# Clustered attention and a gated FFN on one core: Strassen's scheme for four more token tiles, the last product in parts, and 44 casts moved to GpSimd

## The chip, the cores and the metric

One core of a Trainium2 chip. The time is that of one execution on the device, in microseconds (us); a lower number is better. The core has five engines with an instruction queue each: TensorE (PE in the profile; its weight loads are shown apart as PEld), VectorE (DVE), ScalarE (ACT), GpSimd (POOL) and SyncE (SP), which in this kernel starts most DMAs. PE writes to PSUM, eight banks per partition; the other tiles lie in SBUF.

## The reference

The inputs are q, k and v of shape (4 batches, 8 heads, 768 tokens, 64), centroids of shape (8, 16, 64) and the three weight matrices of the FFN. All are float32, and so is the output of 3072 x 512.

```python
q_assign = argmax(q_n @ c_n.T, axis=-1)           # nearest of 16 centroids, by cosine
k_assign = argmax(k_n @ c_n.T, axis=-1)
mask     = q_assign[..., :, None] == k_assign[..., None, :]
scores   = where(mask, scale * q @ k.T, -1e9)
attn     = softmax(scores)                        # over the keys
x        = (attn @ v), heads side by side         # (3072, 512)
out      = (sigmoid(x @ w_gate) * (x @ w_val)) @ w_out   # 512 -> 1536 -> 512
```

So each batch has an attention part and an FFN part, and the last matrix product is (3072 x 1536) by (1536 x 512).

## The kernel before

**Attention.** For each pair of heads, k and q are split in two float16 parts: `hi` is the value cast to float16, and `lo` what the cast left out. The two lie side by side in a tile `hl`, which is turned (transposed) into `T`. In batch 0 and the first pair of batch 1 most of this is placed by hand and turned on PE. For the other eleven pairs (three of batch 1, four of batches 2 and 3 each) `pair_prep` does it: `sp(e, side)` makes `hl` of one head and side, with the cast on DVE (line 1353) and the subtraction on POOL (line 1354); `tn` turns `hl` by a DMA transpose on SP (line 410); `lg` multiplies `T` by the centroids on PE (line 434), `pk` picks the nearest on DVE (lines 449 to 469), and `ot` and `hp` bring the result back under `T` as 16 more rows, by DMAs on SP. Then one matmul of `T` against itself (`sc`, line 788, 384 queries wide) gives masked scores. ACT takes the exponential (`es`, line 793), and three matmuls multiply it by v (`av`, line 811). Such a group of one `sc` and three `av` is a step; there are 384 steps, 96 in each batch. At the end of a head DVE adds a correction and inverts the sum (`t`, `rec`, lines 370 and 372), POOL scales (`xp`, line 375), and a DMA transpose on SP writes `xTb` (line 842), the input of the FFN.

**FFN.** It runs in blocks of 384 tokens, two to a batch. For each of the 12 groups of 128 hidden units, a gate (`g`, line 529, four matmuls) and a value (`v`, line 545, four matmuls) are made; ACT takes tanh, and DVE joins both into `hT` (line 550). The output product has two forms. `plain_out` multiplies one tile of 128 tokens by the whole of w_out: 12 matmuls 512 wide (line 583), then one copy out of PSUM, on ACT or DVE, and one store. `product_out` takes two tiles (`t1`, `t2`) by Strassen's scheme in Winograd's form: instead of eight products of quarter matrices it makes seven, each of six matmuls 256 wide (line 716). It needs sums of the quarters of `hT` (`Sums.make`, lines 626 to 632, DVE, four for a pair) and differences of the quarters of w_out (`mix_wo`, line 276, DVE, eight operations in all). The differences overwrite the tiles `kheld`, `qheld` and `vheld`, which held batch 0's last pair of heads, and a quarter of w_out itself. Its results are added up from two PSUM banks `x` and `y`, which are filled in turn (`end1` to `end7`, line 658 on DVE, one on ACT at line 662). In batch 0 all six tiles go through `plain_out`; in batches 1 to 3 tiles (0, 1) are one pair, and tiles (3, 2) and (4, 5) are two pairs that go through one call.

**Order.** The order of all instructions is fixed when the program is built. `at` and `plan` put a piece of work at a step number plus an offset from the table `SCHED`. FFN matmuls are a queue of small pieces (atoms), each with a cost in ns; at each step `ffn_run(ns)` adds the step's allowance (`ns00` to `ns33`, batch and quarter of the batch) and issues atoms until it is used up. Each engine then runs its own list in order, and waits on semaphores where a tile is not ready or a buffer not free. `sc`, `g`, `v` and most logits share a ring of four PSUM banks; `x` and `y` are the two banks of the pool `op`. After the last step the rest of the queue runs without attention work beside it: the last block's gates and values, and then the product of tiles (3, 2) and (4, 5) of batch 3, with `final` set. In that last call the seven products run back to back, and the stores are made in two column halves, each over both pairs.

Of the kernel before, what the change touches and what calls it, by code (L numbers as in the profile page):

```python
# [98 lines left out]
def kernel(  # L99
# [415 lines left out]
    def ffn_atoms(xT, t0, n, b, final=False):  # L515
        blk = t0 // 384
        gv = []
        cost = NDC * max(n, 80) / 2.4 + 3
        pairs = [] if b < PB else [(0, 1)] if blk == 0 else [(3, 2), (4, 5)]
        sm = {x: Sums(b, *x) for x in pairs}  # L520

        def gate(fc, st):
            def f():
                need(("w", fc // WQ, 0), *(("x", b, p, t0 // 128 + c) for p in range(NP) for c in range(n // 128)))
                if fc == 0:
                    HB[b, blk] = htp.tile([128, NFC, 384], HP, name="hT")
                g = bank(512, name="g")
                for dc in range(NDC):
                    PE.matmul(  # L529
                        out=g[:, 0:n], lhsT=wg[fc // WQ][:, dc, fc % WQ, :],  # L530
                        rhs=xT[:, dc, t0 : t0 + n],
                        start=(dc == 0), stop=(dc == NDC - 1),
                    )
                th = thp.tile([128, 384], FP, name="th")
                ACT.activation(th[:, 0:n], g[:, 0:n], AF.Tanh)  # L535
                st.append(th)

            return f

        def val(fc, st):  # L540
            def f():
                need(("w", fc // WQ, 1))
                w = bank(512, name="v")
                for dc in range(NDC):
                    PE.matmul(  # L545
                        out=w[:, 0:n], lhsT=wv[fc // WQ][:, dc, fc % WQ, :],
                        rhs=xT[:, dc, t0 : t0 + n],
                        start=(dc == 0), stop=(dc == NDC - 1),
                    )
                DVE.scalar_tensor_tensor(  # L550
                    HB[b, blk][:, fc, 0:n], st[0][:, 0:n], 1.0, w[:, 0:n], ALU.add, ALU.mult
                )
                for k, x in SUMS_AT[b >= PB, blk].get(fc, []):
                    sm[x].make(k)
                if fc == NFC - 1 and pairs and blk == 0:
                    aside.extend(product_out(b, [sm[(0, 1)]], False))

            return f

        for fc in range(NFC):  # L560
            st = []
            gv.append((cost, gate(fc, st)))
            gv.append((cost, val(fc, st)))
        outs = []
        if b < PB:
            for t in range(n // 128):
                outs += plain_out(b, blk, t)
        elif blk == 1:
            outs = product_out(b, [sm[x] for x in pairs], final)
        return gv + outs  # L570

    def plain_out(b, blk, t):
# [3 lines left out]
        def outp(part):  # L576
# [22 lines left out]

    PB = 1  # L600
    SUMS_AT = {
        (False, 0): {}, (False, 1): {},
        (True, 0): {5: [(3, (0, 1))], 11: [(1, (0, 1)), (2, (0, 1))]},
        (True, 1): {
            1: [(1, (3, 2))], 5: [(2, (3, 2)), (3, (3, 2))], 6: [(3, (4, 5))],
            11: [(1, (4, 5)), (2, (4, 5))],
        },
# [26 lines left out]
    def product_out(b, sums, final):  # L634


        P_ = len(sums)
        st = {}

        def begin():  # L640
            need(*(("wo", i) for i in range(WOP)), *(("wt", i, c) for i in range(4) for c in range(2)))
            slot = taken["op"] % 2
            u = [out_bank() for _ in range(2)]
            x = 0 if slot != taken["last"] else 1
            taken["last"] = (slot + x) % 2
            taken["pair"] = True
            for z, t in (("x", u[x]), ("y", u[1 - x])):
                st[z] = t[:, 0 : P_ * HD].rearrange("p (e m) -> p e m", m=HD)
            if P_ == 1:
                ob = osp.tile([128, 2, DM], FP, name="ob")  # L650
                st["o1"], st["o2"] = ob[:, 0:1], ob[:, 1:2]
            else:
                st["o1"] = osp.tile([128, 2, DM], FP, name="ob")
                st["o2"] = osp.tile([128, 2, DM], FP, name="ob")
            for o in ("o1", "o2"):
                st[o, 0], st[o, 1] = st[o][:, :, 0:HD], st[o][:, :, HD:DM]

        plus = lambda dst, a, z: DVE.tensor_tensor(dst, a, z, ALU.add)  # L658
        C11, C12, C21, C22 = ("o1", 0), ("o1", 1), ("o2", 0), ("o2", 1)

        def end1():
            ACT.activation(st[C11], st["x"], AF.Copy)

        def end4():
            plus(st[C21], st["y"], st[C11])

        def end6():
            plus(st[C12], st["x"], st[C11])

        def end5():  # L670
            plus(st[C22], st["y"], st[C11])
            for m in sums:
                m.make(4)

        def end7():
            plus(st[C21], st["x"], st[C21])
            plus(st[C22], st["x"], st[C22])
            for i, m in enumerate(sums):
                store(st["o2"][:, i], b, m.t2, 1)

        def end3():
            plus(st[C12], st["y"], st[C12])
            if final:
                store(st[C12], b, sums[0].t1, P_, slice(HD, DM))

        def end2():
            plus(st[C11], st["x"], st[C11])
            taken["pair"] = False
            if final:
                store(st[C11], b, sums[0].t1, P_, slice(0, HD))  # L690
            else:
                store(st["o1"], b, sums[0].t1, P_)

        steps = [
            ("x", lambda m: tok(b, m.t1, 0), B11, True, end1),
            ("y", lambda m: tok(b, m.t2, 1), T4, True, end4),
            ("x", lambda m: m.of[2], T2, True, end6),
            ("y", lambda m: m.of[1], T1, True, end5),
            ("x", lambda m: m.of[3], T3, False, end7),
            ("y", lambda m: m.of[4], B22, False, end3),  # L700
            ("x", lambda m: tok(b, m.t1, 1), B21, True, end2),
        ]
        atoms = []
        G = SCHED.get("og", 3)

        def atom(k, e, g):
            z, lhs, rhs, start, end = steps[k]

            def f():
                if k + e + g == 0:  # L710
                    while aside and P_ > 1:
                        aside.pop(0)[1]()
                    begin()
                a = lhs(sums[e])
                for c in range(g, g + G):
                    PE.matmul(  # L716
                        out=st[z][:, e], lhsT=a[:, c, :], rhs=rhs[:, c, :],
                        start=start and c + e == 0, stop=c == HF - 1, skip_group_check=True,
                    )
                if g + G == HF and e == P_ - 1:  # L720
                    end()

            return f

        for k in range(7):
            for e in range(P_):
                for g in range(0, HF, G):
                    atoms.append((G * (HD / 2.4 + 2.5), atom(k, e, g)))
        return atoms

    queue = []
# [118 lines left out]
    def plan(name, step, f):  # L850
        at(SCHED.get(name, step), f)
# [489 lines left out]
        plan(f"wo{i}", 44 + 6 * i, lambda i=i: load_wo(i))  # L1341
    for i in range(4):
        for c in range(2):
            plan(f"wt{i}{c}", (150 + 8 * i if i < 3 else 200) + 4 * c, lambda i=i, c=c: mix_wo(i, c))

    def pair_prep(b, p, use):
        st = {}

        def sp(e, side):
            if side == 0:  # L1350
                st["hl", e] = hlp.tile([128, 12, 128], HP, tag="hl", name="hl")
            hl, r = st["hl", e][:, 6 * side : 6 * side + 6], RAW["kq"[side], b, p][:, e]
            DVE.tensor_copy(hl[:, :, 0:64], r)  # L1353
            POOL.tensor_tensor(hl[:, :, 64:128], r, hl[:, :, 0:64], ALU.subtract)  # L1354

        def lgt(e):
# [129 lines left out]
```

## Time and profile before

| | |
|---|---|
| median of 3 runs | 324.65 us (324.54 to 325.34) |
| the profiled execution | 324.9 us, of which 323.1 us are its span, from the first to the last instruction |
| PE busy | 314.7 us, 97% of the span |
| DVE busy | 226.7 us, 70% |
| ACT busy | 231.1 us, 72% |
| POOL busy | 108.6 us, 34% |
| TensorE clock granted | full speed in every slice |

A matmul's duration in the profile includes the time that it takes to run out of the array, so two matmuls overlap in the list: what one costs PE is the distance from its start to the start of the next. A bracket behind a row of a timeline says how long the engine was idle before it, and what released it. "x4" behind a row means four instructions merged into it.

### The profile page before, as it was taken

To read this page: it belongs to the slowest core of one execution; us is meant where nothing else is said; L and a number is where in the kernel's file an instruction comes from. 1 tells how busy PE (TensorE), PEld (TensorE's weight loads), DVE (VectorE), ACT (ScalarE), POOL (GpSimd) and SP (SyncE) were. 2 spreads that over 40 slices of the span, in tenths; PEclk is the share of its full clock that TensorE was granted. 3 is DMA by queue.
4 is the path that set the end of the run, shared out by engine and by line. 5 is a ranking of instruction groups with operands and counts; after the bars stand their busy time and mean duration, and the time that the engine had idled before them with its cause. 6 is when DMAs were issued, how large, how long until landed. Compare 5 with 4: busy or idle time off the path is not lost.

```text
span 323.1 us, 9150 instructions
## 1 busy us (share of the span) xinstructions
PE 314.7 (97%) x3504; PEld 222.1 (69%) x3504; DVE 226.7 (70%) x586; ACT 231.1 (72%) x520; POOL 108.6 (34%) x145
## 2 busy tenths in 40 slices
PE   7999999999999999999999999999999999999994
PEld 5888666766766656666777687666777688667683
DVE  6899656777667997576879688576867356555654
ACT  6688988787899978877867866788777876332310
POOL 5887464154335265433132352423111111000000
PEclk9999999999999999999999999999999999999999
DMA  6999995837987996974784741952503012200103
GB/s 203 384 255 189 244 164 114 200 93 222 251 122 185 159 215 155 248 197 90 107 217 115 233 101 42 311 99 52 111 2 95 34 26 79 77 2 1 67 0 130
DMA packets 77675, 45.15 MB, mean 140 GB/s; under 512 B 56832, under 2 KB 75072, under 8 KB 77632
## 3 DMA queue, kind: packets, MB, share of 16 engines
q1 hardware_dynamic: 73664, 39.73, 49.1%
q0 software_dynamic: 3680, 4.72, 8.9%
q8 instruction: 27, 0.44, 0.6%
q10 hardware_dynamic: 288, 0.13, 0.2%
q14 instruction: 16, 0.13, 0.1%
HBM read 28.34 MB, written 6.29 MB: 107 GB/s over the span
## 4 chain that ended last, share of the span: by engine, by line
PE 87%; DVE 5%; issue 3%; DMA 2%; POOL 1%; SPq 0%; ACT 0%; POOLq 0%; DVEq 0%
PE g L529 19%; PE v L545 19%; PE sc L788 17%; PE av L811 10%; PE o L716 10%; PE o L583 4%; PE lg L434 2%; PE oh_ps L1097 1%; PE lg L421 1%; PE t_ps L1037 1%; DMA xTb<-xp 1%; DMA qraw<-in_q_dram 1%; PE wm L879 1%; DVE ob L658 1%; POOL xp L375 1%
## 5 line engine op out<-in xcount | busy, mean ns | idle before, releaser
L793 ACT ACTIVATE es<-sc 128x384 f16<-128x384 f32 x384 | 174.5, 492 | 40.3 <-PE sc L788 30.9
L788 PE MATMUL sc<-T 128*128 128x384 f16 x384 | 117.8, 326 | 1.0 <-DVE lgs L449 0.6
L811 PEld LDWEIGHTS <-es 128*128 128x128 f16 x1152 | 81.3, 98 | 35.8 <-issue 0.7
L811 PE MATMUL av<-va,es 128*128 128x65 f16 x1152 | 97.5, 194 | 0.0
L550 DVE SCALAR_TENSOR_TENSOR hT<-th,v 128x384 f16<-128x384 f32 x96 | 53.1, 553 | 56.2 <-PE av L811 36.8
L529 PE MATMUL g<-xTb,wg 128*128 128x384 f16 x384 | 78.2, 326 | 0.6 <-DMA xTb<-xp 0.5
L545 PE MATMUL v<-xTb,wv 128*128 128x384 f16 x384 | 78.1, 326 | 0.0
L535 ACT ACTIVATE th<-g 128x384 f32<-128x384 f32 x96 | 47.2, 492 | 33.3 <-PE g L529 14.0
L375 POOL TENSOR_TENSOR xp<-t,rec 128x384 f16<-128x384 f32 (+1 forms) x30 | 21.8, 728 | 100.5 <-DVE rec L372 50.0
L529 PEld LDWEIGHTS <-wg 128*128 128x128 f16 x384 | 37.2, 97 | 19.7 <-issue 0.4
L545 PEld LDWEIGHTS <-wv 128*128 128x128 f16 x384 | 37.4, 98 | 19.0
L788 PEld LDWEIGHTS <-T 128*128 128x128 f16 x384 | 37.1, 97 | 0.6 <-DVE T L1118 0.5
L1354 POOL TENSOR_TENSOR hl<-kraw,hl 128x384 f16<-128x384 f32 x22 | 20.2, 920 | 42.2 <-DVE hl L1353 19.6
L658 DVE TENSOR_TENSOR ob<-o,ob 128x256 f32<-128x256 f32 (+1 forms) x42 | 22.6, 551 | 9.7 <-PE o L716 8.9
L716 PEld LDWEIGHTS <-sum 128*128 128x128 f16 x216 | 20.9, 98 | 5.6 <-DVE sum L632 0.7
L716 PE MATMUL o<-wo,hT 128*128 128x256 f16 x162 | 24.0, 272 | 0.2 <-DVE ob L658 0.2
L1354 POOL TENSOR_TENSOR hl<-qraw,hl 128x384 f16<-128x384 f32 x22 | 20.7, 940 | 10.0 <-DVE hl L1353 9.7
L370 DVE TENSOR_TENSOR t<-av,sv 128x390 f32<-128x390 f32 (+1 forms) x30 | 14.4, 479 | 8.0 <-PE av L811 7.8
L583 PE MATMUL o<-wo,hT 128*128 128x512 f16 x72 | 19.9, 379 | 0.0
L716 PEld LDWEIGHTS <-hT 128*128 128x128 f16 x162 | 15.7, 97 | 4.2 <-issue 0.4
L449 DVE TENSOR_REDUCE lgs<-lg 128x192 f32<-128x384 f32 x23 | 12.7, 551 | 2.7 <-PE lg L434 2.6
L322 POOL CAST va<-vraw 128x768 f16<-128x768 f32 x15 | 12.9, 860 | 2.5 <-DMA vraw<-in_v_dram 2.5
(140 smaller groups left out, 321.9 us busy)
## 6 DMA issues: line engine op xcount, KB each, us to landing
vraw<-in_v_dram SPq DMA_DIRECT2D x15, 384.0 KB, 5.2
kraw<-in_k_dram SPq DMA_DIRECT2D x14, 384.0 KB, 4.1
out_dram<-ob SPq DMA_DIRECT2D x20, 256.0 KB, 2.4
qraw<-in_q_dram SPq DMA_DIRECT2D x12, 384.0 KB, 4.4
wg<-in_moe_w_gate_dram POOLq DMA_DIRECT2D x2, 768.0 KB, 9.1
wv<-in_moe_w_val_dram POOLq DMA_DIRECT2D x2, 768.0 KB, 9.9
wo<-in_moe_w_out_dram POOLq DMA_DIRECT2D x2, 768.0 KB, 8.8
T<-ohT SPq DMA_DIRECT2D x44, 24.0 KB, 1.9
```

The source lines that it names most:

```text
L375: (eng or POOL).tensor_tensor(x, t[:, 0:nq, 0:64], bcast(rec[:, 0:nq], 64), ALU.mult)
L529: PE.matmul(out=g[:, 0:n], lhsT=wg[fc // WQ][:, dc, fc % WQ, :], rhs=xT[:, dc, t0 : t0 + n], start=(dc == 0), stop=(dc == NDC - 1),)
L535: ACT.activation(th[:, 0:n], g[:, 0:n], AF.Tanh)
L545: PE.matmul(out=w[:, 0:n], lhsT=wv[fc // WQ][:, dc, fc % WQ, :], rhs=xT[:, dc, t0 : t0 + n], start=(dc == 0), stop=(dc == NDC - 1),)
L550: DVE.scalar_tensor_tensor(HB[b, blk][:, fc, 0:n], st[0][:, 0:n], 1.0, w[:, 0:n], ALU.add, ALU.mult)
L583: PE.matmul(out=o, lhsT=HB[b, blk][:, fc, bass.ts(t, 128)], rhs=wo[fc // WON][:, fc % WON, :], start=(fc == 0), stop=(fc == NFC - 1),)
L658: plus = lambda dst, a, z: DVE.tensor_tensor(dst, a, z, ALU.add)
L716: PE.matmul(out=st[z][:, e], lhsT=a[:, c, :], rhs=rhs[:, c, :], start=start and c + e == 0, stop=c == HF - 1, skip_group_check=True,)
L788: PE.matmul(out=sc.rearrange("p (c t) -> p c t", t=128), lhsT=s["k"], rhs=s["q"], start=True, stop=True,)
L793: ACT.activation(es, sc, AF.Exp, scale=SCALE)
L811: PE.matmul(out=av[:, a0 + s["c0"] + i, :], lhsT=s["es"][:, bass.ts(i, 128)], rhs=VA[b, p][:, e, s["j"], :], start=(first and i == 0 and a ...
L1354: POOL.tensor_tensor(hl[:, :, 64:128], r, hl[:, :, 0:64], ALU.subtract)
```

## The change

Four things are done.

1. Batch 0's second block goes through `product_out`, as in the other batches, and takes tile 2 of the first block with it: tiles (3, 2) and (4, 5) are two pairs. Only tiles 0 and 1 stay with `plain_out`. So that the differences of w_out are there in time, the eight operations of `mix_wo` are planned for steps 108 to 150, where they were at 150 to 170 and at 200 and 204.
2. The very last product (k = 6 of the final call) is done in three parts on banks of the ring instead of on `x`: the first tile whole (six matmuls 256 wide), the second in two column halves (six matmuls 128 wide each). Each part has its own addition and its own store.
3. In `pair_prep` the 44 casts of line 1353 are issued on POOL instead of DVE, just ahead of the subtraction that was on POOL already.
4. The allowances of FFN work per step are changed: 490 to 440 ns in the second half of batch 0, 12 ns more in batch 1, 7 or 8 ns less in batch 2.

```diff
-    300, "ns11": 280, "ns12": 290, "ns13": 265, "ns2": 600, "ns3": 350, "dm0": 7, "dm1": 2,
+    312, "ns11": 292, "ns12": 302, "ns13": 277, "ns2": 600, "ns3": 350, "dm0": 7, "dm1": 2,
...
-    -1, "b1lv1": 0.5, "b1lv2": 0.5, "b1lv3": 1.5, "ns02": 490, "ns03": 490, "ns20": 500,
-    "ns21": 491, "ns22": 481, "ns23": 491, "ns30": 443, "ns31": 443, "ns32": 443, "ns33": 423,
+    -1, "b1lv1": 0.5, "b1lv2": 0.5, "b1lv3": 1.5, "ns02": 440, "ns03": 440, "ns20": 492,
+    "ns21": 484, "ns22": 474, "ns23": 484, "ns30": 443, "ns31": 443, "ns32": 443, "ns33": 423,
...
-        pairs = [] if b < PB else [(0, 1)] if blk == 0 else [(3, 2), (4, 5)]
+        pairs = [(3, 2), (4, 5)] if blk else [] if b < PB else [(0, 1)]
...
-                for k, x in SUMS_AT[b >= PB, blk].get(fc, []):
+                for k, x in SUMS_AT[blk].get(fc, []) if pairs else []:
                     sm[x].make(k)
...
-        if b < PB:
-            for t in range(n // 128):
-                outs += plain_out(b, blk, t)
-        elif blk == 1:
-            outs = product_out(b, [sm[x] for x in pairs], final)
+        if blk == 1:
+            outs = product_out(b, [sm[x] for x in pairs], final)
+        elif b < PB:
+            for t in range(2):
+                outs += plain_out(b, blk, t)
...
         def end2():
             plus(st[C11], st["x"], st[C11])
             taken["pair"] = False
-            if final:
-                store(st[C11], b, sums[0].t1, P_, slice(0, HD))
-            else:
-                store(st["o1"], b, sums[0].t1, P_)
+            store(st["o1"], b, sums[0].t1, P_)
...
+        def closing(e, a, z):
+            def f():
+                o = bank(z - a, name="o_end")
+                lhs = tok(b, sums[e].t1, 1)
+                for c in range(HF):
+                    PE.matmul(
+                        out=o, lhsT=lhs[:, c, :], rhs=B21[:, c, a:z],
+                        start=c == 0, stop=c == HF - 1,
+                    )
+                m = st["o1"][:, e, a:z]
+                plus(m, o, m)
+                store(m.unsqueeze(1), b, sums[e].t1, 1, slice(a, z))
+
+            return f
+
-        for k in range(7):
+        for k in range(6 if final else 7):
             for e in range(P_):
                 for g in range(0, HF, G):
                     atoms.append((G * (HD / 2.4 + 2.5), atom(k, e, g)))
+        if final:
+            for e, a, z in ((0, 0, HD), (1, 0, HD // 2), (1, HD // 2, HD)):
+                atoms.append((900, closing(e, a, z)))
         return atoms
...
-            plan(f"wt{i}{c}", (150 + 8 * i if i < 3 else 200) + 4 * c, lambda i=i, c=c: mix_wo(i, c))
+            plan(f"wt{i}{c}", 108 + 12 * i + 6 * c, lambda i=i, c=c: mix_wo(i, c))
...
-            DVE.tensor_copy(hl[:, :, 0:64], r)
+            POOL.tensor_copy(hl[:, :, 0:64], r)
             POOL.tensor_tensor(hl[:, :, 64:128], r, hl[:, :, 0:64], ALU.subtract)
```

More of the change, by code (lines that the diff above doesn't have):

```diff
@@ L601 @@
     SUMS_AT = {
-        (False, 0): {}, (False, 1): {},
-        (True, 0): {5: [(3, (0, 1))], 11: [(1, (0, 1)), (2, (0, 1))]},
-        (True, 1): {
+        0: {5: [(3, (0, 1))], 11: [(1, (0, 1)), (2, (0, 1))]},
+        1: {
             1: [(1, (3, 2))], 5: [(2, (3, 2)), (3, (3, 2))], 6: [(3, (4, 5))],
```

## The prediction

> **What bounds the kernel now.** I read the page's first two parts, then the busy times of each engine in stretches of 15 us, then the timeline wherever PE was not full. In the second fence the columns behind a stretch are its length and the busy us (and instructions) of PE, PEld, DVE, ACT and POOL.
>
> ```profile
> PE 314.7 (97%) x3504; PEld 222.1 (69%) x3504; DVE 226.7 (70%) x586; ACT 231.1 (72%) x520; POOL 108.6 (34%) x145
> ...
> PE   7999999999999999999999999999999999999994
> ...
> PEclk9999999999999999999999999999999999999999
> ```
>
> ```profile
> 75.00:90.00 15.00, 15.00 (x187) 10.05 (x186) 10.43 (x29) 12.78 (x31) 6.17 (x7) 1.00 0.87 215
> 90.00:105.00 15.00, 15.00 (x181) 10.19 (x179) 10.20 (x31) 13.64 (x33) 7.07 (x8) 1.00 0.83 165
> 105.00:120.00 15.00, 14.43 (x166) 9.29 (x164) 14.47 (x34) 12.74 (x31) 7.27 (x8) 1.00 0.87 193
> 195.00:210.00 15.00, 14.18 (x153) 9.86 (x151) 10.22 (x28) 10.45 (x24) 5.89 (x8) 1.00 0.65 186
> 315.00:323.10 8.10, 3.95 (x34) 2.95 (x32) 3.90 (x7) 0.00 (x0) 0.00 (x0) 1.00 0.35 129
> ```
>
> PE is the bound at its full clock, and almost without a hole: every slice but the first and the last is at 90% or more, and of the stretches from 45 us on only 105 to 120, 195 to 210 and the tail show it less than full (0.57, 0.82 and 4.15 us). So a matmul taken out is time taken out, one for one, and the other edits count only by the few holes that they close or open. ACT is next (13.64 of 15 us), and DVE is all but full in one stretch, 105 to 120, which is where PE waits.
>
> **The product of batch 0 (edit 1).** What one form costs PE is the distance between starts:
>
> ```profile
> 67.88 0.50 PE L920 MATMUL t_ps<-identh,hl 128*128 128x128 f16 x6
> 68.22 1.03 PE L583 MATMUL o<-wo,hT 128*128 128x512 f16 x4
> 69.08 0.26 PE L811 MATMUL av<-va,es 128*128 128x65 f16 x3
> ```
>
> ```profile
> 313.27 1.47 PE L716 MATMUL o<-kheld,sum 128*128 128x256 f16 x12
> 314.58 1.47 PE L716 MATMUL o<-vheld,sum 128*128 128x256 f16 x12
> ```
>
> Four plain matmuls take 69.08 - 68.22 = 0.86 us, 0.215 each; twelve of the product take 314.58 - 313.27 = 1.31, 0.109 each. Out go 4 tiles x 12 = 48 plain ones, 10.32 us. In come 7 products x 2 pairs x 6 = 84, 9.17 us. Term: **-1.15 us**, on PE itself, with nothing to hide it; what new waits could take of it is bounded in the terms below.
>
> Beside it DVE gets eight sums, and six additions out of PSUM in place of one copy (ACT loses three copies and gets one).
>
> ```profile
> L658 DVE TENSOR_TENSOR ob<-o,ob 128x512 f32<-128x512 f32 x21 | 14.1, 688 | 9.6 <-PE o L716 8.9 <-ACT es L793 0.7
> L658 DVE TENSOR_TENSOR ob<-o,ob 128x256 f32<-128x256 f32 x21 | 8.4, 414 | 0.1
> L626 DVE TENSOR_TENSOR sum<-hT 128x768 f16<-128x768 f16 x9 | 5.9, 650 | 0.2
> L1353 DVE CAST hl<-qraw 128x384 f16<-128x384 f32 x22 | 9.8, 447 | 0.0
> L1353 DVE CAST hl<-kraw 128x384 f16<-128x384 f32 x22 | 9.6, 435 | 0.0
> ```
>
> That is at most 8 x 0.65 + 7 x 0.69 - 0.69 = 9.3 us of DVE, against 19.4 us of casts that leave it (edit 3): DVE's total falls by 10 us. The eight `mix_wo` operations are only moved.
>
> **The hole at 115 us (edits 1 and 3 together).**
>
> ```profile
> 114.78 0.25 PE L811 MATMUL av<-va,es 128*128 128x65 f16 x3
> 115.61 0.32 PE L788 MATMUL sc<-T 128*128 128x384 f16 x1 [0.57 <-DVE lgs L449]
> ```
>
> ```profile
> L276 DVE TENSOR_TENSOR kheld<-wo x2: 550/912/1273, 105.7 to 108.0; 128x768 f16<-128x768 f16 x2
> L1353 DVE CAST hl<-kraw x22: 324/354/981, 44.0 to 222.3; 128x384 f16<-128x384 f32 x22
> ```
>
> ```profile
> 113.12 1.07 DVE L276 TENSOR_TENSOR vheld<-wo,wo 128x768 f16<-128x768 f16 x1
> 114.11 0.97 DVE L1353 CAST hl<-qraw 128x384 f16<-128x384 f32 x1
> ```
>
> PE waits for a ring bank that DVE's reduction of the logits has not read yet; DVE is late by a mix of 1.07 us and a cast of 0.97 just ahead of it. Three av take 0.09 us, so the start of `sc` is late by about 0.74 us. In the changed order the cast is gone from DVE and this mix runs earlier. But where do the mixes go? The two of `kheld` stood at steps 150 and 154 and ran at 105.7 and 108.0 us, 0.58 us a step, so step 108 is at about 81 us. There, from 75 to 105 us, about four or five of the new sums fall too: 8 mixes at 0.55 to 1.27 (both from the `kheld` row) and 5 sums at 0.65 add 7.7 to 13.4 us to DVE's 20.6 of 30 us; the casts there go, 30/178 of 19.4 us (they start between 44.0 and 222.3), 3.3. That is 25 to 31 us: 83% to more than full. Bounds: all 0.74 us gained, or the hole comes twice instead of once (+0.74). I take half of the gain, **-0.35 us**: the nearest row is 105 to 120, 96% full, and it cost 0.74 us in one place; the middle of my estimate, 93%, is a little under it.
>
> **The holes at 195 to 207 us.** The longest is a gate that waits for its input.
>
> ```profile
> 200.62 0.65 PE L529 MATMUL g<-xTb,wg 128*128 128x384 f16 x3
> 201.72 0.32 PE L529 MATMUL g<-xTb,wg 128*128 128x384 f16 x1 [0.46 <-DMA xTb<-xp]
> ```
>
> After three gate matmuls (0.49 us) the fourth should start at 201.11; it is late by 0.61. By the order of the changed program, three more product matmuls (0.33 us) stand between the last `av` of that half and this gate, so the wait shrinks by that. Against it, in batch 1 the way from the last `av` to the same gate gets shorter by 12 plain matmuls, 2 `sc` and 6 `av` and longer by 21 of the product: 2.58 + 0.5 - 2.29, about 0.8 us. Batch 1 showed no wait there; its reserve is unknown, and batch 2's lateness of 0.61 is the nearest row for what it could cost. Net **-0.15 us**, between -0.6 and +0.6.
>
> **The casts on POOL (edit 3).**
>
> ```profile
> L893 POOL CAST hl<-qraw x1: 498/498/498, 57.1 to 57.1; 128x384 f16<-128x384 f32 x1
> L1354 POOL TENSOR_TENSOR hl<-qraw,hl 128x384 f16<-128x384 f32 x22 | 20.7, 940 | 10.0 <-DVE hl L1353 9.7
> POOL hl L1354 <- DVE hl L1353: 29.3, 22, 7.6
> ```
>
> A cast of this shape took 0.50 us on POOL; 44 are 22 us, and POOL goes from 34% to about 41% of the span. Each stands right ahead of its subtraction, and POOL sat idle ahead of these subtractions for 29.3 us in 22 places waiting for DVE's cast, so most casts fall into idle time. Behind them in POOL's queue wait `xp` (and through it `xTb` and the gates), the casts of v, and through `hl` SP's transposes, with the hops and loads behind those. The closest pair that I found:
>
> ```profile
> 122.18 1.47 SPq L410 DMA_TRANSPOSE T<-hl  x1
> 126.91 0.46 PE L434 MATMUL lg<-cm,T 128*128 128x32 f16 x12
> DMA to landing us min/median/max: 3.2/4.1/6.4
> ```
>
> From this transpose to the logits that need it are 4.73 us, against 4.1 for a median landing: 0.6 us of slack, if the median holds. Its subtraction ended at 120.71 (119.80 + 0.91, below), 1.5 us ahead, so 0.5 us more on POOL reach neither. I cost the casts at **0**; what hides them is POOL's idle time, and without that cover a pair costs up to 4 x 0.5 = 2 us of delay less the slack. Bounds: -0.3 (transposes start earlier) to +1.5.
>
> ```profile
> 119.80 0.91 POOL L1354 TENSOR_TENSOR hl<-qraw,hl 128x384 f16<-128x384 f32 x1 [0.30 <-DVE hl L1353]
> ```
>
> DVE operations with two inputs in SBUF are stretched at times when POOL is at work: the `kheld` row above has 0.55 and 1.27 us for one shape. The Trainium skill's page "SBUF — State Buffer", section "Who interferes with whom", speaks against the edit: a DVE instruction with two SBUF inputs and a GpSimd instruction that reads SBUF exclude each other for the whole instruction. By that rule each cast moved can hold up a sum, a mix or a v sum by all of its 0.5 us, while the casts that leave DVE stop being held. The trace agrees with a wait of that size, since 1.27 - 0.55 = 0.72 is less than one POOL subtraction (0.94); I leave the sum as it is and let the rule weigh for the first rival below.
>
> **The last product in parts (edit 2).**
>
> ```profile
> 316.00 1.48 PE L716 MATMUL o<-wo,sum 128*128 128x256 f16 x12
> 317.66 1.47 PE L716 MATMUL o<-wo,hT 128*128 128x256 f16 x12 [0.18 <-DVE ob L658]
> 319.17 0.69 DVE L658 TENSOR_TENSOR ob<-o,ob 128x512 f32<-128x512 f32 x1 [0.96 <-PE o L716]
> 319.89 0.38 SPq L502 DMA_DIRECT2D out_dram<-ob  x1
> 317.64 2.63 SPq L502 DMA_DIRECT2D out_dram<-ob  x4
> ```
>
> The last product waits for DVE to read bank `x`: 317.66 - 316.00 - 1.31 = 0.35 us; on ring banks it doesn't. Its length stays: 6 x 0.109 + 12 x 0.056 (six 128 wide ones took 68.22 - 67.88) = 1.33 us. The last addition shrinks from 0.69 to about 0.28 us (414 less half of 688 - 414 for half the width). So the last sum would be ready at 319.86 - 0.35 - 0.41 = 319.1. But SP has three stores to issue there instead of one. Three are issued from 317.64 on before them; at 0.38 us each (the last one's row) to an assumed 0.45, six in a row end at 319.9 to 320.3, where the old last one ended at 320.27. So the SP queue takes back nearly all of the 0.76 us, and what stays is that the last store has 64 KB instead of 256. Bounds: 0 to -0.7. I take **-0.25 us**.
>
> **Allowances (edit 4).** They only move where FFN pieces stand between steps; PE is full on both sides. Taken at 0, bounds -0.3 to +0.5 (ACT at 13.64 of 15 us is the cover that could go).
>
> **Sum.** -1.15 - 0.35 - 0.15 - 0.25 = -1.9 us against the profiled 324.9: 323.0. The median of the runs lies 0.25 lower, at 324.65, so the forecast is **322.75 us**, 0.6% faster. A change under 0.3%, about 1 us, can't be told from none here.
>
> **The rivals.**
>
> *The saving is handed back on DVE.* The mixes and sums between 80 and 105 us, stretched beside a busier POOL, repeat the hole of 115 us once or twice (0.74 each), and batch 1's gate waits 0.6: -1.9 + 0.74 + 0.6, about 324.1, within 0.3%. For it: the 83% to more than full above. Against: PE stood full from 75 to 105 us, and the mixes are spread over 24 us.
>
> *POOL makes it slower.* The mechanism is POOL's queue: four casts more in each pair push the subtractions past the slack of 0.6 us, and PE waits at the logits. With 22 transposes, it outweighs the -1.9 us from 0.09 us a transpose on, and gives a measurable loss from 0.13; at 0.2 us, 4.4 in all, it would be 327.1. For it: POOL and SP run in order. Against: POOL's 41%, the idle time of 29.3 us, and the 1.5 us at the closest place.
>
> *More than summed.* DVE's relief closes the holes at 115 and at 195 to 207 (1.3 us) and SP's stores don't hold the tail (0.7): 324.65 - 1.15 - 0.74 - 0.9 - 0.6 = 321.3.
>
> **How the numbers follow.** The forecast gets 0.65 (its own range 322.0 to 323.6), the hand-back 0.16, POOL 0.07 and the larger gain 0.12. The range runs from 321.4, near the larger gain, to 324.4, just past the hand-back; POOL's case and some of the larger gain are left out. Faster is the forecast, the larger gain and a little of the hand-back: 0.80; same 0.13; slower 0.07.
>
> **What would show it.** Right: 48 fewer matmuls at line 583 and 84 more at the product; PE full from 45 us on; the wait for `lgs` gone; product seven starting 1.31 us after the sixth; the last store issued at about the same distance from the sixth product as before. Wrong: PE waits for `T` or `xTb` at the start of heads or blocks, or for a ring bank held by `lgs` between 80 and 105 us, or `sum` late at the new product.

## The result and the profile after

The changed kernel takes 330.47 us (median of 4 runs, 329.33 to 330.88) against 324.6 for the kernel before in the same session: a ratio of 1.0173, 95% interval 1.0154 to 1.0192. It is 1.7% slower where 0.6% faster was forecast. The profiled execution took 330.49 us, with a span of 328.3.

The page's first two parts, and the stretches in the columns of the prediction's fence:

```profile
PE 314.7 (96%) x3546; PEld 224.4 (68%) x3546; DVE 225.8 (69%) x558; ACT 231.1 (70%) x518; POOL 129.6 (39%) x189
...
PE   7899999999998999899999999999999999999995
```

```profile
75.00:90.00 15.00, 14.22 (x172) 9.16 (x169) 11.46 (x27) 12.00 (x27) 7.96 (x10) 1.00 0.62 178
90.00:105.00 15.00, 14.34 (x165) 9.26 (x163) 12.64 (x27) 12.17 (x29) 8.79 (x11) 1.00 0.69 155
105.00:120.00 15.00, 13.92 (x179) 10.53 (x178) 12.76 (x30) 12.14 (x29) 6.38 (x10) 1.00 0.70 140
120.00:135.00 15.00, 13.47 (x174) 10.53 (x171) 12.47 (x31) 10.94 (x25) 10.55 (x16) 1.00 0.67 156
195.00:210.00 15.00, 14.36 (x173) 11.36 (x171) 12.22 (x29) 9.92 (x21) 7.19 (x11) 1.00 0.49 135
```

PE's busy time is the same 314.7 us in a span 5.2 us longer (the granted clock is 1.00 in every stretch shown). From 75 to 105 us, where it stood full, it now lacks 1.44 us, and from 105 to 135 another 2.6. No other engine is the new bound: from 75 to 120 us ACT has less work in each stretch than before, and DVE is at most 85% full. The time lies in many waits for single operations. Four of them, from PE's timeline:

```profile
80.34 0.34 PE L802 MATMUL sc<-T 128*128 128x384 f16 x1 [0.49 <-DVE T L997]
...
106.24 0.32 PE L802 MATMUL sc<-T 128*128 128x384 f16 x1 [1.08 <-DVE hT L550]
...
132.03 0.65 PE L529 MATMUL g<-xTb,wg 128*128 128x384 f16 x3
133.88 0.32 PE L529 MATMUL g<-xTb,wg 128*128 128x384 f16 x1 [1.20 <-DMA xTb<-xp]
...
209.37 0.32 PE L545 MATMUL v<-xTb,wv 128*128 128x384 f16 x1 [0.64 <-DVE hT L550]
```

To compare kernels I add up such **holes**: the distance from one matmul's start to the next, less the median distance of that kind of matmul in the kernel before, wherever the excess is over 0.04 us. (The gate above: three matmuls from 132.03 at 0.163 us, so the fourth is due at 132.52 and comes 1.36 late.) The startup, 0 to 45 us, is left out: the same matmul at its end starts at 43.9 to 44.8 us in these profiles, at 44.47 before and at 44.43 after. The table gives the rest, in us, from one profile of each kernel. Each ratio is to the kernel before in the same session, whose median was 324.3 to 324.9 us; across sessions the ratios compare better than the medians.

| kernel | 45–75 | 75–120 | 120–165 | 195–240 | tail | sum after 45 | median us | ratio, 95% interval |
|---|---|---|---|---|---|---|---|---|
| before | 0.07 | 0.99 | 0 | 1.50 | 0.45 | 3.0 | 324.6 | 1 |
| after | 0.77 | 4.07 | 3.01 | 1.54 | 0.10 | 9.5 | 330.47 | 1.0173 [1.0154, 1.0192] |
| e1: edit 3 alone | 0.63 | 0.66 | 1.06 | 1.79 | 0.45 | 4.6 | 325.95 | 1.0045 [1.0030, 1.0061] |
| e2: all but edit 3 | 0.94 | 3.12 | 2.01 | 0.50 | 0.10 | 6.7 | 327.21 | 1.0087 [1.0071, 1.0104] |
| e3: edit 2 alone | 0.07 | 0.99 | 0 | 1.15 | 0.10 | 2.3 | 324.19 | 0.9989 [0.9975, 1.0003] |
| e4: edit 4 alone | 0.93 | 1.95 | 0.24 | 0.07 | 0.45 | 3.7 | 325.63 | 1.0031 [1.0016, 1.0046] |
| e10: e2, no sums or differences in batch 0 | 0.94 | 1.15 | 2.20 | 0.50 | 0.10 | 4.9 | 326.05 | 1.0044 [1.0025, 1.0064] |
| e16: after, picks as reductions | 0.77 | 2.82 | 2.29 | 0.87 | 0.10 | 6.9 | 328.30 | 1.0131 [1.0098, 1.0163] |
| e17: e2, picks as reductions | 0.94 | 2.98 | 1.43 | 0.51 | 0.10 | 6.0 | 327.24 | 1.0086 [1.0069, 1.0103] |

The holes grew by 6.5 us after 45 us. The matmuls that edit 1 saves take 1.2 us of that back (PE's last matmul starts at 324.23 us, where it was 318.86), and 5.2 to 5.6 us remain in the span and the time.

### The profile page after: what moved, and what is told of

Same layout as the page of the kernel before. It is cut to its first block, busy times and chain, and to the rows that moved or that the text cites. A ratio compares the mean times of both kernels' runs of the same rounds, so it can differ in the third digit from the quotient of the medians.

```text
span 328.3 us, 9203 instructions
## 1 busy us (share of the span) xinstructions
PE 314.7 (96%) x3546; PEld 224.4 (68%) x3546; DVE 225.8 (69%) x558; ACT 231.1 (70%) x518; POOL 129.6 (39%) x189
## 4 chain that ended last, share of the span: by engine, by line
PE 81%; DVE 9%; DMA 3%; ACT 2%; issue 2%; POOL 1%; SPq 1%; DVEq 0%
PE v L545 18%; PE g L529 17%; PE sc L802 16%; PE o L712 13%; PE av L825 9%; DVE hT L550 2%; DMA kraw<-in_k_dram 2%; PE lg L434 2%; PE o L583 1%; ACT es L807 1%; DMA xTb<-xp 1%; PE lg L421 1%; DVE oh L462 1%; PE t_ps L1051 1%; POOL hl L1030 1%
## 5 line engine op out<-in xcount | busy, mean ns | idle before, releaser
L657 DVE TENSOR_TENSOR ob<-o,ob 128x512 f32<-128x512 f32 (+1 forms) x48 | 26.5, 566 | 10.2 <-PE o L712 7.9
L712 PEld LDWEIGHTS <-sum 128*128 128x128 f16 x264 | 25.7, 98 | 6.3 <-DVE sum L631 0.2
L712 PE MATMUL o<-wo,hT 128*128 128x256 f16 x186 | 28.4, 272 | 0.0
L712 PEld LDWEIGHTS <-hT 128*128 128x128 f16 x186 | 18.0, 97 | 4.8 <-issue 0.2
L388 POOL TENSOR_TENSOR xp<-t,rec 128x384 f16<-128x384 f32 x8 | 6.6, 825 | 17.9 <-DVE rec L387 15.0
```

Of the source, the lines that this page charges most:

```text
L712: PE.matmul(out=st[z][:, e], lhsT=a[:, c, :], rhs=rhs[:, c, :], start=start and c + e == 0, stop=c == HF - 1, skip_group_check=True,)
```

## Experiments: each edit by itself

Two theories stood at this point. P: the casts on POOL cost the time, by POOL's queue or by holding up DVE. D: the additional DVE work of edit 1 costs it. The letters of later theories (Q, K, QU, H) are explained where they come up in the expectations. The first runs split the change.

**e1: edit 3 alone, on the kernel before.**

```diff
-            DVE.tensor_copy(hl[:, :, 0:64], r)
+            POOL.tensor_copy(hl[:, :, 0:64], r)
```

> The kernel before with edit 3 alone: the 44 casts on POOL, nothing else. Theory P (the casts on POOL are what cost the time, by POOL's queue and by holding up DVE): 327.5 to 330 us. Theory D (the loss comes from edit 1's mixes and sums, bunched on DVE between 80 and 130 us): 324.0 to 325.3, the same as before, and the hole at 115 us smaller.

**e2: the changed kernel without edit 3** (the same line turned back).

> The changed kernel with edit 3 undone: the casts are back on DVE, edits 1, 2 and 4 stand; PE's list is the same. Theory P: 322.5 to 323.7 us, the gain that was forecast. Theory D: 329 to 332, since DVE has the mixes, the sums and 19 us of casts; PE's holes from 75 to 107 us stay at 3 us or more.

Measured: 325.95 us for e1 (1.0045) and 327.21 for e2 (1.0087). Both lie outside the ranges of both theories: neither P nor D alone explains the loss. The casts cost about 1.5 us alone. Beside the other edits they cost 2.8 us by the ratios (1.0173 against 1.0087), or 3.3 by the medians (330.47 - 327.21). The other edits, forecast to gain, cost 2.8 us without the casts. In e1, one hole is a wait for the turned `hl`; the chain of waits ahead of it and PE's timeline:

```profile
113.81 0.46 POOL hl L1353
...
114.34 1.10 POOL hl L1354
115.44 0.77 POOL va L322
116.22 0.49 POOL hl L1353
...
116.77 0.92 POOL hl L1354
...
117.72 5.20 DMA T<-hl
```

```profile
122.96 0.47 PE L434 MATMUL lg<-cm,T 128*128 128x32 f16 x12 [0.79 <-DMA T<-hl]
```

From the kernel before, POOL's and SP's queues and PE at the same work:

```profile
115.17 0.91 POOL L1354 TENSOR_TENSOR hl<-qraw,hl 128x384 f16<-128x384 f32 x1 [0.29 <-DVE hl L1353]
...
116.11 1.89 SPq L410 DMA_TRANSPOSE T<-hl  x1
...
121.47 0.46 PE L434 MATMUL lg<-cm,T 128*128 128x32 f16 x12
```

Before, POOL's subtraction ended at 116.08 and the transpose started at 116.11: this pair has no reserve ahead of the transpose, and 5.36 us from there to the logits against a landing of 5.20 in e1. In e1 two POOL casts of 0.5 us stand in that chain, the transpose starts at 117.72, and PE loses 0.95 us. This much of the casts' cost is POOL's queue.

**e3: edit 2 alone.**

```diff
-        for k in range(7):
+        for k in range(6 if final else 7):
...
+        if final:
+            for e, a, z in ((0, 0, HD), (1, 0, HD // 2), (1, HD // 2, HD)):
+                atoms.append((900, closing(e, a, z)))
```

> The kernel before with edit 2 alone: the last product in three parts. Both theories: 323.9 to 324.5 us; PE's wait before the last product (0.35 us) gone, the last store issued at most 0.2 us earlier because SP issues three where it issued one. If SP doesn't hold it: 323.8 or less.

Measured: 324.19 us, 0.9989 [0.9975, 1.0003]. The interval just takes in no change; the hole of the tail went (0.45 to 0.10), and the gain of about 0.35 us by the ratio is near the 0.25 forecast. In the changed kernel, from PE's timeline and SP's queue:

```profile
321.64 1.49 PE L712 MATMUL o<-wo,sum 128*128 128x256 f16 x12
322.96 1.49 PE L726 MATMUL o_end<-wo,hT 128*128 128x256 f16 x18
...
323.28 2.85 SPq L502 DMA_DIRECT2D out_dram<-ob  x6
```

The last product starts 1.32 us after the sixth, and SP issues six stores in a row for 2.85 us, 0.475 each. The last issue ends 4.49 us after the sixth product's start (4.27 before), so the queue takes back what PE gained; the span ends 6.7 us after that start, where it was 7.1.

**e4: edit 4 alone.**

```diff
-    300, "ns11": 280, "ns12": 290, "ns13": 265, ...
+    312, "ns11": 292, "ns12": 302, "ns13": 277, ...
...
-    ... "ns02": 490, "ns03": 490, "ns20": 500, "ns21": 491, "ns22": 481, "ns23": 491, ...
+    ... "ns02": 440, "ns03": 440, "ns20": 492, "ns21": 484, "ns22": 474, "ns23": 484, ...
```

> The kernel before with edit 4 alone, the changed allowances. Theory Q (the FFN pieces now stand where ACT and the ring of four banks hold PE, whatever DVE does): 326 to 328 us, with holes of 0.2 to 0.5 us between 85 and 110 us. Theory D (DVE's additional work): 324.0 to 325.5.

Measured: 325.63 us, 1.0031 [1.0016, 1.0046], just below theory Q's range and above theory D's. Edit 4 is not free. The holes grow by 0.9 us from 45 to 75 us, in the second half of batch 0, which has 440 ns of FFN a step for 490, and by 1.0 us from 75 to 120 us, which is batch 1 (its first step is at 73.3 us before and 71.5 in e4) with 12 ns more. They shrink by 1.43 us from 195 to 240, around the end of batch 2. In batch 0, with less FFN work between two steps, the steps follow each other faster (its last 48 take 35.9 us for 37.5), while DVE and ACT owe the same work for each. That this makes the holes there is argued, not shown, and what makes those of batch 1 stays open.

## Experiments: the second half of batch 0

**e5: the changed kernel, the eight differences as memsets on DVE** (the differences are left out).

```diff
-        DVE.tensor_tensor(o[:, c], a[:, c], z[:, c], ALU.subtract)
+        DVE.memset(o[:, c], 0.0)
```

> The changed kernel with each of the eight mixes replaced by a memset of the same tile on DVE, at the same place in the order (the differences of w_out are left out, so the products are of zeros): no input is read, and it is shorter. Theory D: 1.5 to 3 us faster than the changed kernel, 327.5 to 329, holes from 75 to 107 us at least halved. Theory P: within 0.7 us of the changed kernel.

Measured: 329.48 us, 1.0167 [1.0134, 1.0200], between the two forecasts. 75 to 120 us falls from 4.07 to 3.18: the hole of 1.25 us at 105 goes, the others stay. What the differences read is not the main cost.

**e10: e2 with batch 0's product fed without sums and differences**, which are left out for batch 0; the differences stand at their old steps.

```diff
+            if self.b == 0:
+                self.of[i] = tok(0, self.t2 if i == 1 else self.t1, 0)
+                return
...
+        U1, U2, U3, U4 = (T1, T2, T3, T4) if b else (B11, B21, B22, B12)
...
-            plan(f"wt{i}{c}", 108 + 12 * i + 6 * c, lambda i=i, c=c: mix_wo(i, c))
+            plan(f"wt{i}{c}", (150 + 8 * i if i < 3 else 200) + 4 * c, lambda i=i, c=c: mix_wo(i, c))
```

> The changed kernel with the casts on DVE, in which batch 0's product takes plain quarters of hT and of w_out in place of the eight sums and the differences (left out for batch 0, so its last four tiles are not the reference's), and the mixes stand where they stood before; PE's list keeps its order and shapes. It differs from the run with the casts back on DVE (327.2) by DVE's preparation alone. Theory D: 323.0 to 325.0 us, holes from 75 to 107 us below 0.8. Theory Q: 326 to 327.5.

Measured: 326.05 us, 1.0044 [1.0025, 1.0064]: inside theory Q's range by the time, while the holes from 75 to 120 us fell nearly as D expected. The stretch from 75 to 120 us in e2 and then in e10:

```profile
75.00:120.00 45.00, 43.37 (x518) 29.68 (x516) 39.26 (x94) 36.90 (x86) 17.58 (x20) 1.00 0.65 166
```

```profile
75.00:120.00 45.00, 44.65 (x544) 31.32 (x542) 34.71 (x90) 38.73 (x90) 18.43 (x21) 1.00 0.75 170
```

DVE has 4.6 us less to do, PE lacks 0.35 us instead of 1.63, and the holes fall from 3.12 to 1.15. So in these profiles 2.0 us of holes are DVE's preparation of the new product, at a DVE that is 87% full in e2. By the ratios e10 gains 1.4 us on e2; its profile is the fastest of its ten executions, 324.99 us. The profile puts five of e2's eight waits of over 0.15 us there down to ACT (1.5 us in all) and three to DVE; two of the five are left in e10, so DVE's lateness seems to reach PE by way of ACT too. What remains in e10 at 120 to 165 us (2.20) is not batch 0's preparation.

**e11: e2 with six differences at steps 64 to 89 and two at 112 and 117.**

```diff
-            plan(f"wt{i}{c}", 108 + 12 * i + 6 * c, lambda i=i, c=c: mix_wo(i, c))
+            plan(f"wt{i}{c}", (64 + 10 * i if i < 3 else 112) + 5 * c, lambda i=i, c=c: mix_wo(i, c))
```

> The changed kernel with the casts on DVE, and six of the eight mixes at steps 64 to 89, the last two at 112 and 117. Theory D: 325.0 to 326.5 us, since DVE's work is spread wider. Theory Q: 326.8 to 327.5, as with the mixes in their place.

Measured: 327.24 us, 1.0076 [1.0051, 1.0101], the same as e2 within the intervals and not the gain that D forecast. The holes from 75 to 120 fall by 1.6 us and those from 45 to 75 rise by 1.2: the cost moves with the work.

**e8: the changed kernel with batch 1's old allowances.**

```diff
-    312, "ns11": 292, "ns12": 302, "ns13": 277,
+    300, "ns11": 280, "ns12": 290, "ns13": 265,
```

> The changed kernel with batch 1's allowances as before (300, 280, 290, 265): by the order of its list, matmuls of 7.05 us instead of 5.30 stand between the last av of batch 1's first half and the fourth gate matmul. If the hole of 1.36 us at 132 us is the short way to that gate: it goes, and the time is 328.8 to 329.6. If it is DVE's late t and rec, which only move along: above 330.

Measured: 328.75 us, 1.0114 [1.0082, 1.0145], 1.7 us better than the changed kernel; from 120 to 165 us the holes fall from 3.01 to 1.25, and the late gate of 1.36 us is gone. Other places move too: from 195 to 240 us the holes fall from 1.54 to 0.28, and from 75 to 120 they rise from 4.07 to 4.64. The chain of waits of the changed kernel shows what that gate waited for:

```profile
128.07 1.28 DVE ob L657 x2
129.35 0.28 DVE t L370
...
129.65 0.19 DVE rec L372
...
129.91 0.51 POOL xp L375
...
130.44 3.39 DMA xTb<-xp
...
133.88 0.32 PE g L529
```

Two additions of the new product stand on DVE ahead of a correction in batch 1's first half, and behind it come POOL and a transpose of 3.39 us. The correction starts 2.04 us after the last `av` that it needs (127.23 and 129.27 us), where it was 0.58 before (123.82 and 124.40). In e8 it starts 1.10 us after that `av`, but PE has 6.85 us of work from there to the gate, where the changed kernel has 5.3. By these numbers the hole hangs on both, a late input and a short way.

## Experiments: why the casts cost

Theory K: POOL's reads of SBUF hold DVE operations with two inputs there. Theory QU: the casts cost by their time in POOL's queue. Both are tried on e2, which has its casts on DVE, with one more operation of the casts' shape on POOL ahead of each subtraction.

**e12: a memset (reads nothing). e13: a cast (reads `raw`).** Each writes the half of `hl` that the subtraction writes over.

```diff
             DVE.tensor_copy(hl[:, :, 0:64], r)
+            POOL.memset(hl[:, :, 64:128], 0.0)
```

```diff
             DVE.tensor_copy(hl[:, :, 0:64], r)
+            POOL.tensor_copy(hl[:, :, 64:128], r)
```

> The changed kernel with the casts on DVE, and on POOL in place of each a memset of the half of hl that the subtraction overwrites: POOL is as busy in its queue, but the added operation reads nothing. Theory QU (the casts cost by their place in POOL's queue, ahead of subtractions, transposes and xp): 329.3 to 330.5 us, like the changed kernel. Theory K (they cost because an operation of POOL that reads SBUF holds up DVE's operations with two inputs): 326.7 to 328.0, as with the casts back on DVE, and the means of DVE's lines 462 and 469 stay near 0.255 and 0.19 us.

> As the run with the memset, but the added operation is a cast of the same raw tile into that half: the same place in the queue, and it reads SBUF. Both theories: slower than with the casts on DVE alone, 329 to 332 us. Theory K: at least 1.5 us slower than with the memset, and the means of lines 462 and 469 above 0.30 us. Theory QU: within 0.7 us of the memset.

Measured: 330.14 us for the memset, 1.0174 [1.0145, 1.0204], inside QU's range, and 329.24 for the cast, 1.0139 [1.0111, 1.0166]. What reads nothing costs as much as what reads, so K falls as the whole explanation. A part of it stands: the comparisons of the picks, with two inputs, went from 287 ns in e2 to 301 beside the memset and to 327 beside the cast. Nor does this prove QU. By shapes, DVE's groups of e2 and then of e12 (busy us, mean ns):

```profile
L1367 DVE CAST hl<-qraw 128x384 f16<-128x384 f32 x22 | 11.2, 511 | 0.0
...
L625 DVE TENSOR_TENSOR sum<-hT 128x768 f16<-128x768 f16 x11 | 6.7, 607 | 0.2
```

```profile
L1367 DVE CAST hl<-qraw 128x384 f16<-128x384 f32 x22 | 13.8, 628 | 0.0
...
L625 DVE TENSOR_TENSOR sum<-hT 128x768 f16<-128x768 f16 x11 | 7.5, 684 | 0.2
```

DVE's own casts, which have one input, are longer beside a memset: DVE operations were held in e12 too. Twelve of these casts end 0.21 us after the end of a memset. This is not the changed kernel's way, which has no such casts on DVE. The changed kernel's timelines of DVE and POOL, ahead of its longest hole, say how:

```profile
102.83 1.45 DVE L462 TENSOR_TENSOR oh<-lgs,mx 128x96 f16<-128x96 f32 x2
104.31 0.89 DVE L469 TENSOR_SCALAR oh<-oh 128x96 f16<-128x96 f16 x1
...
105.64 0.55 DVE L550 SCALAR_TENSOR_TENSOR hT<-th,v 128x384 f16<-128x384 f32 x1
```

```profile
102.19 0.50 POOL L1367 CAST hl<-qraw 128x384 f16<-128x384 f32 x1
102.77 0.92 POOL L1368 TENSOR_TENSOR hl<-qraw,hl 128x384 f16<-128x384 f32 x1
103.63 0.54 POOL L1367 CAST hl<-kraw 128x384 f16<-128x384 f32 x1
104.25 0.91 POOL L1368 TENSOR_TENSOR hl<-kraw,hl 128x384 f16<-128x384 f32 x1
```

The scaling of the pick (line 469, one input, one output) takes 0.19 us alone. Here it starts after POOL's subtraction has, and ends at 105.20, 0.04 us after the subtraction's end at 105.16. In the changed kernel it is long five times among 22 (0.78 to 0.89 us beside subtractions, 0.37 beside a cast), and each time it ends 0.04 or 0.05 us after the POOL operation that had started before it; the same in e1, five times. The two comparisons ahead of it (line 462, two inputs, 0.25 us alone) are held as well: they end at 103.80 and 104.28 us, each 0.11 us after a POOL operation. In the kernel before, none of these picks took over 0.26 us. There, 22 subtractions waited for DVE's cast (29.3 us in all), which kept the pairs on POOL apart, while here they run back to back. `hT` behind the pick is late, and `sc` waits for its bank.

**e16: the changed kernel with the picks as reductions; e17: the same on e2, as the control.** The comparison and the scaling become reductions over an axis of length one, on the same tiles, so what they compute is left out. POOL's queue is the same.

```diff
+            if nh == 1:
+                DVE.tensor_reduce(o[:, 0], lg[:, a:z].rearrange("p c (n x) -> p c n x", x=1), AX.X, ALU.max)
+                if not key:
+                    DVE.tensor_reduce(o[:, 0], o[:, 0].rearrange("p c (n x) -> p c n x", x=1), AX.X, ALU.max)
+                continue
             DVE.tensor_tensor(
```

> The changed kernel with the two comparisons and the scaling of each pick (lines 462 and 469) replaced by reductions over an axis of length one, the same number of operations on the same tiles, so that what they compute (which key is the largest) is left out. In the trace of the changed kernel the scaling takes 0.19 us alone and 0.78 or 0.89 when a subtraction on POOL has started before it, and ends then 0.04 us after the end of that subtraction, five times out of five; it has one input and one output. Theory H (a DVE operation is held by the POOL operation beside it, and that is what the casts cost): a reduction is not held, so the long places at 104.3, 152.1 and 208.1 us go, and with them the holes of PE behind them (1.25, 0.39 and 0.80 us, of which the first may keep half); 328.3 to 329.2 us, and no reduction of these over 0.35 us. Theory QU (the casts cost by standing in POOL's queue ahead of subtractions, transposes and xp): the order and lengths on POOL are the same, so 330.0 to 330.9 us.

> The same replacement in the changed kernel without edit 3 (the casts on DVE), as the control: there no pick was long but two of the comparisons, so both theories expect it within 0.5 us of that kernel's 327.2. Theory H: the distance to the run above shrinks from 3.3 us to 1 to 2 us; theory QU: it stays at about 3.3 us.

Measured: 328.30 us for e16, at the lower end of H's range, and 327.24 for e17, as both theories had it. Between these two the casts cost 1.1 us by the medians, where it was 3.3, and 1.5 by the ratios, where it was 2.8; the holes after 45 us differ by 0.9 us, where it was 2.8. From DVE's, POOL's and PE's timelines of e16, at the same place:

```profile
102.49 0.40 DVE L463 TENSOR_REDUCE oh<-lgs 128x96 f16<-128x96 f32 x2
102.92 0.25 DVE L465 TENSOR_REDUCE oh<-oh 128x96 f16<-128x96 f16 x1
...
104.05 0.54 DVE L555 SCALAR_TENSOR_TENSOR hT<-th,v 128x384 f16<-128x384 f32 x1
```

```profile
102.55 0.91 POOL L1373 TENSOR_TENSOR hl<-qraw,hl 128x384 f16<-128x384 f32 x1
103.41 0.56 POOL L1372 CAST hl<-kraw 128x384 f16<-128x384 f32 x1
```

```profile
104.75 0.26 PE L830 MATMUL av<-va,es 128*128 128x65 f16 x3
104.84 0.33 PE L807 MATMUL sc<-T 128*128 128x384 f16 x1
105.00 0.26 PE L830 MATMUL av<-va,es 128*128 128x65 f16 x3
```

POOL runs the same pair, the picks take 0.65 us instead of 2.34, and PE has no hole. This pair shows theory H: the holding of the picks is about half to two thirds of what the casts cost. The share is rough, since e16's interval is wide (1.0098 to 1.0163), but the spans of its four executions, 325.8 to 326.8 us, all lie below the changed kernel's, 327.5 to 328.6. Comparisons and scalings were replaced together, so the share of each is not known. The rule that fits is in the Trainium skill's page "SBUF — State Buffer", section "Who interferes with whom": a VectorE cast or tensor-scalar can run in a mode that takes the port pair shared with GpSimd, whichever of the two engines issues first keeps the pair for the whole instruction, and a reduction never takes it. These traces agree: the held scalings end within 0.05 us of POOL's operation, DVE's casts in e12 were held by memsets too, and no reduction in place of a pick was long in e16 (242 and 253 ns mean, none over 254).

**e15: edit 2 with batch 2's allowances of edit 4 alone**, the two parts that had shown a gain.

```diff
-    ... "ns20": 500, "ns21": 491, "ns22": 481, "ns23": 491,
+    ... "ns20": 492, "ns21": 484, "ns22": 474, "ns23": 484,
...
-        for k in range(7):
+        for k in range(6 if final else 7):
```

> The kernel before with edit 2 and with the allowances of batch 2 alone (7 or 8 ns less a step). In the run with all allowances the holes at 195 to 207 us (1.3 us) were gone, and in the run with edit 2 alone 0.35 us of the tail. If both hold: 322.6 to 323.6 us, faster than both kernels. If the holes only went because batches 0 and 1 were shifted too: 324.0 to 324.4.

Measured: 323.91 us, 0.9973 [0.9959, 0.9986]. It is faster than both kernels, though less so than if both gains had held in full (322.6 to 323.6): its profile keeps 0.64 us of holes from 195 to 240 us, where edit 2 alone leaves 1.15 and edit 4 alone 0.07.

## Why the prediction was wrong, step by step

Three steps failed: the price of DVE's additional work (-0.35 us, where the holes from 75 to 120 us grew by 3.1, of which sums and differences are 2.0), the casts (0, where they cost about 3 us) and the allowances (0, where they cost 1.0). The terms one by one:

- **PE's columns (-1.15): right.** 42 more matmuls are 84 in, 48 out and 6 for the parts of the last product. The last matmul starts 5.4 us later and the holes grew by 6.5, so without holes PE's list is 1.2 us shorter, as counted. It was the only large term that depended on nothing else.
- **The hole at 115 us (-0.35, bounds -0.74 to +0.74): wrong in sign and size.** That hole did close. But 75 to 120 us went from 0.99 to 4.07 us of holes. The step took DVE's load, 83% to more than full, and priced its lateness by one row, at 105 to 120; it came as eight waits of over 0.15 us, not as one. Of the 3.1 us, e4 shows about 1.0 from the allowances, and e2 against e10 2.0 from sums and differences; the casts add 0.95 (4.07 - 3.12). These don't add exactly; e11 shows one way to that: a wait that is removed at one place can come back at another.
- **"DVE's total falls by 10 us": wrong.** It fell by 0.9 (226.7 to 225.8). The picks alone took back 5.3 (2.6 and 2.7), as DVE's groups show by shapes, before and after:

```profile
L462 DVE TENSOR_TENSOR oh<-lgs,mx 128x96 f16<-128x96 f32 x42 | 9.0, 255 | 0.7
...
L469 DVE TENSOR_SCALAR oh<-oh 128x96 f16<-128x96 f16 x22 | 4.2, 189 | 0.8
```

```profile
L462 DVE TENSOR_TENSOR oh<-lgs,mx 128x96 f16<-128x96 f32 x42 | 11.6, 316 | 0.7
...
L469 DVE TENSOR_SCALAR oh<-oh 128x96 f16<-128x96 f16 x22 | 6.9, 314 | 0.8
```

- **The holes at 195 to 207 us (-0.15): inside the bounds, by luck** (1.50 to 1.54 from 195 to 240, by changes that cancel). e4 all but closed them, e2 kept 0.50, and the casts put 1.0 back. The same step's batch 1 gate is where its bound failed: late by 1.36 us, where 0.61 was the nearest row. The step counted PE's way to that gate and not DVE's additions on the way of its input.
- **The casts on POOL (0, bounds -0.3 to +1.5): wrong.** The "closest pair" was not the closest: the pair just ahead of it, at 116.11, had no reserve. And the cover, POOL's idle time, was the wrong thing to count. That idle time had kept POOL's operations apart, and no pick was long beside them; with e1's casts alone, picks were. Alone the casts cost 1.5 us, at the bound; beside the other edits about 3. Of the page of the Trainium skill the step weighed only what it says of two inputs, and the comparisons of line 462 were not among its cases; what the page says of casts and scalings with one input bore on line 469 and was left out.
- **The last product (-0.25): right**, about 0.35 by e3's ratio, whose interval just takes in no change, with SP's queue as the limit, as put.
- **Allowances (0, bounds -0.3 to +0.5): wrong.** +1.0 us by e4's ratio, in parts of opposite sign. "PE is full on both sides" says nothing of the reserve behind it. That ACT's and DVE's work per step stays when the step gets shorter may be the reason from 45 to 75 us; for 75 to 120 us the cause is open.
- **The rivals.** The first, the saving handed back on DVE, had the mechanism, the place and the reason (a busier POOL), and its two waits of 0.74 and 0.6 were too few. The second had POOL as the cause and the wrong path: it counted the queue, and the queue made one hole of 0.95 us in e1, while beside the other edits the larger part was the holding. Neither reached 330, since each was worked out as if the others didn't happen.

The long wait at 132 us hangs on DVE's additions and on PE's shorter way, and goes with batch 1's old allowances, but what of the 2.2 us from 120 to 165 in e10 each of them makes was not separated. What the casts cost beyond the holding of the picks, 1.1 to 1.5 us, was not taken apart either. Nor was a version tried with the sums and differences moved off DVE.

## What to carry to other kernels

An engine that is full for 30 us on end isn't proof of a reserve behind it: before work is added to the engines that feed it, find the smallest slack in each place where they hand over, and price lateness by the number of such places. Waits of an engine off the path can be what keeps it out of another's way; moving work into them removes the pacing, so look at which operations on the neighbour are short only because they run in those gaps. Split a change of several edits into its parts: here edit 2 and batch 2's allowances gained 0.9 us (324.6 times 0.0027), and the rest lost over 6.

## What the runs showed of the hardware that was not expected

- A DVE operation with one input and one output (0.19 us alone) took 0.78 to 0.90 us where a POOL subtraction had started before it, and ended 0.04 or 0.05 us after it, nine times in two kernels. A DVE reduction on the same tile took 0.25 us beside the same POOL work.
- DVE's comparisons with two inputs (0.25 us alone) took 0.48 to 0.98 us beside POOL casts and subtractions, six times in the changed kernel, and ended 0.11 us after them.
- A POOL memset of 128x384 float16, which reads nothing, cost about as much time in 44 places (330.14 us) as a cast of the same size that reads SBUF (329.24), and twelve DVE casts beside it ended 0.21 us after its end.
